# Values scaled by the positive softmax sum as they leave PSUM, and a new written-out order, in a linear-attention and SwiGLU block

## Chip, cores and metric

The kernel runs on one core of one Trainium2 chip. The metric is the device time of one execution in microseconds; lower is better. A launch is repeated and the median is taken.

## What is computed

One transformer block with conditioning: 2048 tokens of 512 numbers, bf16. Six vectors of 512 come from a small product with `c` and set scale, shift and gate of both halves. The first half is linear attention with 32 heads of 16, whose feature map is a pair of softmaxes over 16 numbers; the second is a SwiGLU feed-forward of width 1376.

```python
    mod = (_silu(c) @ w_mod).reshape(c.shape[0], 6, 1, -1)
    h = _layernorm(x, axis=-1) * (1 + ca) + sa
    # attention on h: q, k, v = split(h @ wqkv) in 32 heads of 16
    pq = jnp.einsum('bhsd,hdf->bhsf', q, w_phi)
    pk = jnp.einsum('bhsd,hdf->bhsf', k, w_phi)
    phi_q = jnp.concatenate([_softmax(pq, axis=-1), _softmax(-pq, axis=-1)], axis=-1)
    phi_k = jnp.concatenate([_softmax(pk, axis=-1), _softmax(-pk, axis=-1)], axis=-1)
    kv = jnp.einsum('bhsf,bhsd->bhfd', phi_k, v)
    z = jnp.einsum('bhsf->bhf', phi_k)
    num = jnp.einsum('bhqf,bhfd->bhqd', phi_q, kv)
    den = jnp.einsum('bhqf,bhf->bhq', phi_q, z)[..., None] + 1e-06
    o = num / den
    # x = x + ga * (o @ wo); then the same norm with cb, sb, and
    # x = x + gb * ((silu(h @ w_gate) * (h @ w_up)) @ w_down)
```

## The kernel before

The 2048 tokens are 16 tiles of 128 (`NT`), in four chunks of 512 columns. The two weights `wq` and `wk` are first multiplied by the block-diagonal matrix of `w_phi` (`fold_phi`, L507): each 128-row block is transposed (`wk` on TensorE, L518; `wq` by a DMA transpose through `transposed`, L292, into `WT`), multiplied (L529) and written back (L532, L533).

**First norm.** `first_norm` (L541) takes statistics on VectorE (L348, L349), the reciprocal root (`rstd_lnexp`, on ScalarE L377 or GpSimd L381) and normalizes x to `xn` (L392 to L398). `first_T` (L556) turns `xn` so that the 512 features lie on the partitions, `hT`, and applies scale and shift. Chunk 0 is turned on TensorE, two tiles at a time (`modulate_T`, L403); chunks 1 to 3 by DMA transposes into `raw` (L563), with the scaling after it on VectorE, ScalarE or GpSimd (L571 to L575).

**Key side.** `k_tile` (L595) makes, for one tile, K (L602) and V (L606) in PSUM. ScalarE writes exp(K) and exp(-K) side by side to `e` (L613), 1024 numbers a token. V is copied out of PSUM to `va` with a constant column of ones behind each of eight groups of 64 (L619). VectorE sums `e` in groups of 16 to S, 64 sums a token (L623); R is 1/S, by VectorE (L629) or as exp(-ln S) on ScalarE (L627, L628); GpSimd multiplies all of `e` by R (L631). `kv_tile` (L635) then adds the tile's product of `e` with `va` to an accumulator in PSUM, in eight groups of 65 columns (L638), 64 of values and one of z. After all tiles `f_kvz` (L746) masks it to `KVZ`.

**Query side.** `q_tile` (L653) does the same for Q (L661, L665, L669) but keeps the positive half unscaled, and multiplies the negative half by the ratio of the two sums, `Rq` (L671 to L677), since `o` is a quotient. A DMA transpose puts it into `pT` (L681). `attend_tile` (L773) multiplies `pT` with `KVZ` (L782), divides (L785, L786); `turn`, `project` (L815) with `wo` (scaled by the gate, L738), the residual (L818) and the second norm follow; then the feed-forward: `ffn_gu` (L867, L874, L877, L883), `ffn_tail` (L907, L917), `ffn_down` (L939, L950, L954), output L959.

**What sets the order.** The kernel doesn't issue as it is written. Each step is recorded as an operation with one to three alternatives (engine, cost in the planner's us, function). `ORDER` is a written-out list of the number 4 x operation + alternative: it says in which order operations are given their places and which engine takes each. `Plan.run` (L168) goes through it with the costs, puts each operation at a start, chooses the buffer slots, and issues all in the order of these starts. An engine works through its queue in that order. SyncE's queue (called XBAR) holds all loads and all DMA transposes, at most eight under way at a time. An alternative marked `DVE*` is also kept clear of GpSimd. PSUM is two banks of accumulator and six single banks that all steps share. Where TensorE would pause, `fill` (L989) puts in matmuls on a tensor of ones whose result isn't used (L1006).

## Time and profile before

| what | value |
|---|---|
| median of 13 runs | 207.28 us (205.28 to 208.26) |
| profiled execution, device time | 207.72 us |
| its span, first to last instruction | 205.9 us |
| TensorE busy | 194.3 us, 94% |
| VectorE busy | 143.1 us, 69% |
| GpSimd busy | 127.4 us, 62% |
| ScalarE busy | 109.2 us, 53% |
| first K product on TensorE starts | 14.41 us |

A page of the profile lists engines as PE (TensorE matmuls), PEld (their weight loads), DVE (VectorE), ACT (ScalarE), POOL (GpSimd) and SP (SyncE; SPq is its queue of DMA issues). L602 is line 602 of the kernel. A group such as `one_ps<-wk,hT 128x512 x64` names what is written and read, the shape and the count; behind it stand the busy time, the mean of one in ns, and the idle time of the engine just before, with what ended it. Matmuls overlap, so a group's length on PE is more than the time it takes from the next one; the distance of starts tells that. The chain that ended last is followed back from the last instruction through what released each step.

### The profile page before, as it was taken

Reading aid. Unit: us, or ns where it says so; the run is one execution under the profiler, and the core shown is the slowest. Engines: PE = TensorE matmul, PEld = TensorE weight load, DVE = VectorE, ACT = ScalarE, POOL = GpSimd, SP = SyncE. Lnnn points to the kernel's source line nnn. Section 1 sums busy time; section 2 is a strip of 40 time slices with the busy share of each in tenths; the row PEclk is TensorE's granted clock in tenths of the full one; section 3 lists DMA queues with packets and bytes.
Section 4 is the critical chain, followed back from the end, with each engine's and each line's share of the span. In section 5 each row is a group of like instructions: output and inputs, shape, how many; then the busy total and the mean of one; then the engine's idle time right before and its main releaser. Section 6 shows DMA issues by size and latency. Waiting matters only on the chain.

```text
span 205.9 us, 4577 instructions
## 1 busy us (share of the span) xinstructions
PE 194.3 (94%) x1761; PEld 131.5 (64%) x1761; DVE 143.1 (69%) x284; ACT 109.2 (53%) x221; POOL 127.4 (62%) x180
## 2 busy tenths in 40 slices
PE   7499889999887999999999999999999999999994
PEld 3274365545353597788667866578768688765852
DVE  7699978999998899999987976855324141150533
ACT  2199989999697785456425443425224134332310
POOL 3488986889794767798896585646450860240242
PEclk9999999999999999999999999999999999999999
DMA  5999999994217647483938855041100000101212
GB/s 159 381 376 253 266 193 309 212 377 151 47 29 76 127 80 133 97 148 63 181 76 155 105 99 121 3 103 37 51 29 0 25 30 0 38 16 38 74 31 64
DMA packets 52136, 24.47 MB, mean 119 GB/s; under 512 B 43313, under 2 KB 48914, under 8 KB 52114
## 3 DMA queue, kind: packets, MB, share of 16 engines
q1 hardware_dynamic: 51968, 24.11, 49.9%
q8 instruction: 14, 0.23, 0.5%
q10 hardware_dynamic: 146, 0.07, 0.1%
q14 instruction: 8, 0.07, 0.1%
HBM read 11.58 MB, written 2.10 MB: 66 GB/s over the span
## 4 chain that ended last, share of the span: by engine, by line
PE 65%; DMA 11%; ACT 7%; POOL 5%; DVE 5%; SPq 3%; issue 3%; DVEq 0%; POOLq 0%; ACTq 0%
PE one_ps L867 29%; PE one_ps L939 18%; DMA pT<-eq 6%; PE one_ps L815 6%; DMA wk<-in_A_wqkv_dram 3%; ACT e L613 3%; PE one_ps L661 3%; PE one_ps L907 2%; PE one_ps L602 2%; POOL e L631 2%; ACT hT L573 2%; ACT va L619 2%; POOL eq L677 2%; PE kv_ps L782 1%; SPq L292 1%
## 5 line engine op out<-in xcount | busy, mean ns | idle before, releaser
L867 PE MATMUL one_ps<-hT,wgu_sb 128*128 128x256 bf16 (+1 forms) x800 | 75.6, 251 | 0.1
L867 PEld LDWEIGHTS <-wgu_sb 128*128 128x128 bf16 x800 | 65.5, 98 | 9.2 <-issue 0.2
L874 ACT ACTIVATE sg<-one_ps 128x512 bf16<-128x512 f32 (+1 forms) x42 | 23.5, 573 | 37.1 <-PE one_ps L867 30.5
L939 PE MATMUL one_ps<-wd_sb,gu 128*128 128x512 bf16 (+2 forms) x176 | 39.9, 372 | 0.0
L883 POOL TENSOR_TENSOR gu<-usb,sg 128x512 bf16<-128x512 bf16 x16 | 18.8, 1178 | 33.3 <-ACT usb L881 21.4
L877 DVE TENSOR_TENSOR gu<-one_ps,sg 128x512 bf16<-128x512 f32 (+1 forms) x26 | 16.6, 639 | 26.6 <-PE one_ps L867 12.3
L631 POOL TENSOR_TENSOR e<-e,R 128x1024 bf16<-128x1024 bf16 x16 | 31.0, 1956 | 5.3 <-DVE R L629 4.6
L939 PEld LDWEIGHTS <-gu 128*128 128x128 bf16 (+1 forms) x187 | 17.8, 98 | 16.0
L950 DVE TENSOR_TENSOR fg<-one_ps,gab 128x512 bf16<-128x512 f32 (+1 forms) x16 | 10.6, 665 | 17.6 <-PE one_ps L939 17.6
L348 DVE BATCH_NORM_STATS2 st<-x_c 128x6 f32<-128x512 bf16 x32 | 21.4, 681 | 1.8 <-DMA x_c<-in_A_x_dram 1.6
L669 DVE TENSOR_REDUCE Sq<-eq 128x64 f32<-128x1024 bf16 x16 | 19.0, 1191 | 0.0
L881 ACT CAST usb<-one_ps 128x512 bf16<-128x512 f32 x16 | 9.4, 585 | 17.8 <-PE one_ps L867 17.8
L623 DVE TENSOR_REDUCE S<-e 128x64 f32<-128x1024 bf16 x16 | 18.6, 1184 | 0.1
L665 ACT ACTIVATE eq<-one_ps 128x512 bf16<-128x512 f32 x32 | 17.2, 624 | 1.8 <-PE one_ps L661 1.8
L613 ACT ACTIVATE e<-one_ps 128x512 bf16<-128x512 f32 x32 | 17.6, 659 | 0.1
L677 POOL TENSOR_TENSOR eq<-eq,Rq 128x512 bf16<-128x512 bf16 x15 | 15.8, 1059 | 0.9 <-DVE Rq L672 0.5
L815 PE MATMUL one_ps<-wo_sb,oT 128*128 128x512 bf16 x64 | 15.8, 379 | 0.0
L606 PE MATMUL one_ps<-wv,hT 128*128 128x512 bf16 x64 | 15.8, 379 | 0.0
L602 PE MATMUL one_ps<-wk,hT 128*128 128x512 bf16 x64 | 15.6, 379 | 0.0
L661 PE MATMUL one_ps<-wq,hT 128*128 128x512 bf16 x64 | 15.4, 379 | 0.0
L818 DVE TENSOR_TENSOR x_c<-x_c,one_ps 128x512 bf16<-128x512 bf16 x16 | 10.9, 680 | 5.9 <-PE one_ps L815 5.8
L954 POOL TENSOR_TENSOR ot<-x_c,fg 128x512 bf16<-128x512 bf16 x8 | 9.2, 1152 | 7.5 <-DVE fg L950 7.5
(113 smaller groups left out, 261.8 us busy)
## 6 DMA issues: line engine op xcount, KB each, us to landing
wmod_sb<-in_w_mod_dram SPq DMA_DIRECT2D x2, 1024.0 KB, 7.3
out_dram<-ot SPq DMA_DIRECT2D x15, 128.0 KB, 1.9
...
```

Of the source, the lines that this page charges most:

```text
L348: pl.op("DVE", r=reads, w=[st6], us=0.6, fn=lambda: nc.vector.bn_stats(st6()[:], src))
L602: nc.tensor.matmul(pk()[:], lhsT=hT[c_i][k][:, cols], rhs=Wk2[:, k, :], start=(k == 0), stop=(k == KD - 1))
L613: nc.scalar.activation(e()[:, :, sg].rearrange("p g h f -> p g (h f)"), pk()[:].rearrange("p (g n) -> p g n", g=G), ACT.Exp, scale=(1.0, - ...
L631: pl.op("POOL", r=[e, R], w=[e], us=1.92, fn=lambda: nc.gpsimd.tensor_tensor(e()[:].rearrange("p g s h f -> p (g s h) f"), e()[:].rearrang ...
L661: nc.tensor.matmul(pq()[:], lhsT=hT[c_i][k][:, cols], rhs=Wq2[:, k, :], start=(k == 0), stop=(k == KD - 1))
L669: pl.op("DVE", r=be, w=[Sq], us=1.14, fn=lambda: nc.vector.tensor_reduce(Sq()[:].rearrange("p g s h -> p (g s h)"), eq[:].rearrange("p g s ...
L677: eng.tensor_tensor(eq[:, :, 1], eq[:, :, 1], Rq()[:].unsqueeze(3).to_broadcast([P, G, 4, DH]), op=ALU.mult)
L815: nc.tensor.matmul(a()[:], lhsT=oT()[:, j0 + j, :], rhs=wo_sb[:, j, :], start=(j == 0), stop=(j == KD - 1))
L867: nc.tensor.matmul(ps_()[0:fsz, q * n:(q + 1) * n], lhsT=wgu_sb[:, k, i, m * P:m * P + fsz], rhs=h2[k], start=(k == 0), stop=(k == KD - 1))
L874: pl.op("ACT", r=[g, btab], w=[sg], us=0.08 + 0.41 * L / CW, fn=lambda: nc.scalar.activation(sg()[0:fsz, 0:L], g()[0:fsz, 0:L], ACT.Silu))
L883: pl.op("POOL", r=[usb, sg], w=[gu], us=0.17 + 0.98 * L / CW, fn=lambda: nc.gpsimd.tensor_tensor(gu()[0:fsz, 0:L], usb()[0:fsz, 0:L], sg() ...
L939: nc.tensor.matmul(fp()[:], lhsT=b()[0:fsz, c0:c0 + P], rhs=wd_[0:fsz, m, wcs], start=(m == 0), stop=(m == FM - 1))
```

## The change

- **Key side.** V is multiplied by R of the positive half (1/S+) as it leaves PSUM, on VectorE, instead of being copied; the four columns of z behind each group become R of the positive half (copied on GpSimd or ScalarE) instead of one constant column. The positive half of `e` stays as it is; GpSimd multiplies only the negative half, by S+ x R-, which a small product on GpSimd makes first. The quotients are the same. The accumulator's groups have 68 columns instead of 65, and `f_kvz` reads four z columns per group.
- **First loads and first norm.** x of chunk 0 comes in one load instead of two, x of chunk 1 in two instead of one. Chunk 0 is turned tile by tile (`turn_tile`) and `hT` of chunk 0 is tracked tile by tile; the first two tiles of chunk 1 are turned on TensorE as well instead of by a DMA transpose.
- **Planner's costs.** DMA sizes and the costs of DMA transposes are changed, `Rq` (the product) has only GpSimd as an alternative.
- **Order.** `ORDER` is a new list throughout, so places, engines and slots of all steps are dealt anew. By count of the built program: the 64-wide R, 13 on VectorE and 3 on ScalarE before, are all on ScalarE; SyncE issues x of chunk 1 (first half), x of chunk 0, `w_phi`, `wk`, modulation, x of chunk 1 (second half), modulation, `wq`, x of chunk 2, `wv`, two transposes of `wq`, x of chunk 3, the other two. Before, it was x0a, `w_phi`, x0b, x1, `wk`, two modulation loads, x2, `wv`, x3, `wq`, and transposes after that.

```diff
--- before.py
+++ after.py
@@ -39,51 +39,51 @@
-PAIRS = (0, 1)
-DMA_LN1 = (1, 2, 3)
+DMA_LN1 = 6
 FILL_FROM, FILL_TO, FILL = 1.3, 90.0, 0.85
 
 
 ORDER = [
-    0, 44, 48, 8, 52, 20, 28, 56, 4, 12, 148, 68, 100, 116, 16, 132, 76, 72, 64, 172, 80, 164, 85, 256, 176, 36, 168, 88, 180, 60, 152, 98, 248, 94,
...
+    20, 44, 0, 48, 8, 56, 4, 64, 148, 12, 52, 264, 272, 116, 164, 24, 268, 276, 16, 168, 280, 172, 76, 176, 68, 181, 284, 290, 80, 72, 152, 294, 60,
...
@@ -124,7 +124,7 @@
     OWN = {"PE": 0.0, "DVE": 0.19, "ACT": 0.19, "POOL": 0.12, "SP": 0.0, "XBAR": 0.0, "NONE": 0.0}
-    DMA = (1.9, 385e3, 0.5)
+    DMA = (1.9, 385e3, 0.5, 0.7, 1.3, 1.0)
     LANES = 8
@@ -190,8 +190,8 @@
             elif o.eng == "XBAR" and o.kb == 0:
-                dma = max(dma, o.end + 0.1) + 0.5
-                o.end = max(o.end, dma + 0.6)
+                dma = max(dma, o.end + 0.1) + self.DMA[4 if o.alt[1] > 1.32 else 3]
+                o.end = max(o.end, dma + self.DMA[5])
             elif o.kb < 0:
@@ -316,7 +316,7 @@
     gul_t = [const.tile([P, 2, P], BF16, name=f"gul{i}") for i in range(slots["gul"])]
-    va_t = [const.tile([P, G, HG + 1], BF16, name=f"va{i}") for i in range(slots["va"])]
+    va_t = [const.tile([P, G, NDW], BF16, name=f"va{i}") for i in range(slots["va"])]
     bm4 = const.tile([P, HG], FP32, name="bm4")
@@ -324,9 +324,6 @@
             nc.gpsimd.memset(t[:, :, lastf:P], 0.0)
-        for t in va_t:
-            nc.gpsimd.memset(t[:, :, HG:HG + 1], 1.0)
-
         nc.gpsimd.tensor_tensor(bm4[:], bm128[:, 0:4, :].rearrange("p c f -> p (c f)"),
@@ -338,7 +335,7 @@
     bwgu = [Buf(), Buf()]
-    bc, bphi = Buf(at=2.5), Buf()
+    bc, bphi = Buf(at=2.75), Buf()
     bWq2 = [Buf() for _ in range(KD)]
@@ -428,17 +425,17 @@
-    later(x_ch[0][:, 0:2, :], x_v[0][:, 0:2, :], bx[0:2], 256)
-    later(Wk2[:], wqkv_v[:, :, D:2 * D], bwk[0:1], 594)
-    later(wphi_sb[:], A_w_phi.rearrange("h (q t) f -> (h q) (t f)", t=4), [bphi], 200)
+    later(x_ch[0][:], x_v[0], bx[0:4], 512)
+    later(Wk2[:], wqkv_v[:, :, D:2 * D], bwk[0:1], 560)
+    later(wphi_sb[:], A_w_phi.rearrange("h (q t) f -> (h q) (t f)", t=4), [bphi], 80)
     for k in (0, 2):
         later(wmod_sb[:, k:k + 2, 0:2 * D], wmod_v[:, k:k + 2, 0:2 * D], bm1[k:k + 2], 512)
-    later(x_ch[0][:, 2:4, :], x_v[0][:, 2:4, :], bx[2:4], 256)
-    later(wv_sb[:], wqkv_v[:, :, 2 * D:3 * D], [bwv], 594)
-    later(x_ch[1][:], x_v[1], bx[4:8], 512)
-    later(Wq2[:], wqkv_v[:, :, 0:D], bwq[0:1], 594)
+    later(x_ch[1][:, 0:2, :], x_v[1][:, 0:2, :], bx[4:6], 256)
+    later(x_ch[1][:, 2:4, :], x_v[1][:, 2:4, :], bx[6:8], 256)
+    later(wv_sb[:], wqkv_v[:, :, 2 * D:3 * D], [bwv], 560)
+    later(Wq2[:], wqkv_v[:, :, 0:D], bwq[0:1], 640)
     for c_i in (2, 3):
-        later(x_ch[c_i][:], x_v[c_i], bx[c_i * TPC:(c_i + 1) * TPC], 512)
+        later(x_ch[c_i][:], x_v[c_i], bx[c_i * TPC:(c_i + 1) * TPC], 540)
@@ -502,7 +499,7 @@
     bmask = Buf()
-    pl.op("POOL", w=[bmask], us=1.2, fn=f_masks)
+    pl.op("POOL", w=[bmask], us=0.6, fn=f_masks)
@@ -533,7 +530,7 @@
     hT = [[attn.tile([P, CW], BF16, name=f"hT_{c_i}_{j}") for j in range(KD)] for c_i in range(NCH)]
-    bhT = [[[Buf() for _ in range(KD)] for _ in range(2 if c_i in PAIRS else 1)] for c_i in range(NCH)]
+    bhT = [[[Buf() for _ in range(KD)] for _ in range((4, 2, 1, 1)[c_i])] for c_i in range(NCH)]
@@ -553,14 +550,33 @@
+    def turn_tile(xn, parts, q, t):
+        tp = bank("T", [P, KD, P], BF16)
+
+        def ft():
+            for j in range(KD):
+                nc.tensor.transpose(tp()[:, j, :], xn()[:, q, j * P:(j + 1) * P], ident_b[:])
+        pl.op("PE", r=[xn, parts[q]], w=[tp], us=0.224, fn=ft)
+        for jp in range(2):
+            def evac(act, jp=jp):
+                for j in (2 * jp, 2 * jp + 1):
+                    d = hT[0][j][:, t * P:(t + 1) * P]
+                    if act:
+                        nc.scalar.activation(d, tp()[:, j, :], ACT.Identity, bias=modA[:, j:j + 1], scale=modA[:, KD + j:KD + j + 1])
+                    else:
+                        nc.vector.tensor_scalar(d, tp()[:, j, :], modA[:, KD + j:KD + j + 1], modA[:, j:j + 1],
+                                                op0=ALU.mult, op1=ALU.add)
+            pl.op([("ACT", 0.6, lambda evac=evac: evac(True)), ("DVE", 0.5, lambda evac=evac: evac(False))],
+                  r=[tp, bmodA], w=bhT[0][t][2 * jp:2 * jp + 2])
+
     def first_T(n0, w):
         c_i, t = divmod(n0, TPC)
-        if c_i in DMA_LN1:
+        if n0 >= DMA_LN1:
             raw = sb("prep", "raw1", [P, TPC, KD, P], BF16)
             parts = [Buf() for _ in range(w // 2)]
             for q in range(w // 2):
                 xn, ps2, _ = bxn1[n0 + 2 * q]
-                pl.op("XBAR", r=[xn] + ps2, w=([raw] if q == 0 else []) + [parts[q]], us=1.8, fn=lambda q=q, xn=xn: nc.sync.dma_start(
+                pl.op("XBAR", r=[xn] + ps2, w=([raw] if q == 0 else []) + [parts[q]], us=1.4, fn=lambda q=q, xn=xn: nc.sync.dma_start(
                     raw()[:, 2 * q:2 * q + 2].rearrange("p q j m -> p (q j) m"), xn()[:].rearrange("p q m -> p (q m)"), transpose=True))
@@ -574,9 +590,13 @@
                             d, s, ab, sh, op0=ALU.mult, op1=ALU.add), j))],
-                      r=[raw] + parts + [bmodA], w=[bhT[c_i][t // 2 if c_i in PAIRS else 0][j]])
+                      r=[raw] + parts + [bmodA], w=[bhT[c_i][(t, t // 2, 0, 0)[c_i]][j]])
             return
-        bd = bhT[c_i][t // 2 if c_i in PAIRS else 0]
+        if c_i == 0:
+            for q in range(w):
+                turn_tile(*bxn1[n0 + q], t + q)
+            return
+        bd = bhT[c_i][t // 2]
         for jp in range(2):
@@ -586,11 +606,11 @@
-    bphik, bva, kv_ops = {}, {}, []
+    bphik, bva, bz_, kv_ops = {}, {}, {}, []
         c_i, t = divmod(i, TPC)
-        return bhT[c_i][t // 2 if c_i in PAIRS else 0]
+        return bhT[c_i][(t, t // 2, 0, 0)[c_i]]
@@ -615,31 +635,35 @@
         bva[i] = Buf("va", lambda slot: va_t[slot])
-        def fva(copy):
-            copy(bva[i]()[:, :, 0:HG], v()[:].rearrange("p (g d) -> p g d", g=G))
-        pl.op([("ACT", 0.48, lambda: fva(nc.scalar.copy)), ("DVE", 0.6, lambda: fva(nc.vector.tensor_copy))],
-              r=[v], w=[bva[i]])
-        Ss, R = sb("kph", "S", [P, 2 * H], FP32), sb("kph", "R", [P, 2 * H], FP32)
+        Ss, R = sb("kph", "S", [P, G, 2, 4], FP32), sb("kph", "R", [P, G, 2, 4], FP32)
         pl.op("DVE", r=[e], w=[Ss], us=1.14, fn=lambda: nc.vector.tensor_reduce(
-            Ss()[:], e()[:].rearrange("p g s h f -> p (g s h) f"), axis=AX.X, op=ALU.add))
+            Ss()[:].rearrange("p g s h -> p (g s h)"), e()[:].rearrange("p g s h f -> p (g s h) f"), axis=AX.X, op=ALU.add))
         def fr():
             nc.scalar.activation(R()[:], Ss()[:], ACT.Ln)
             nc.scalar.activation(R()[:], R()[:], ACT.Exp, scale=-1.0)
         pl.op([("DVE", 0.46, lambda: nc.vector.reciprocal(R()[:], Ss()[:])), ("ACT", 0.52, fr)], r=[Ss], w=[R])
+        bz = bz_[i] = Buf()
+        pl.op("POOL", r=[R, Ss], w=[Ss], us=0.22, fn=lambda: nc.gpsimd.tensor_tensor(
+            Ss()[:, :, 0], Ss()[:, :, 0], R()[:, :, 1], op=ALU.mult))
+        pl.op("DVE", r=[v, R], w=[bva[i]], us=0.65, fn=lambda: nc.vector.tensor_tensor(
+            bva[i]()[:, :, 0:HG].rearrange("p g (h d) -> p g h d", d=DH), v()[:].rearrange("p (g h d) -> p g h d", g=G, d=DH),
+            R()[:, :, 0].unsqueeze(3).to_broadcast([P, G, 4, DH]), op=ALU.mult))
+        pl.op([("POOL", 0.17, lambda: nc.gpsimd.tensor_copy(bva[i]()[:, :, HG:NDW], R()[:, :, 0])),
+               ("ACT", 0.24, lambda: nc.scalar.copy(bva[i]()[:, :, HG:NDW], R()[:, :, 0])),
+               ("DVE*", 0.1, lambda: nc.vector.tensor_copy(bva[i]()[:, :, HG:NDW], R()[:, :, 0]))], r=[R, bva[i]], w=[bz])
         bphik[i] = e
-        pl.op("POOL", r=[e, R], w=[e], us=1.92, fn=lambda: nc.gpsimd.tensor_tensor(
-            e()[:].rearrange("p g s h f -> p (g s h) f"), e()[:].rearrange("p g s h f -> p (g s h) f"),
-            R()[:].unsqueeze(2).to_broadcast([P, 2 * H, DH]), op=ALU.mult))
+        pl.op("POOL", r=[e, Ss], w=[e], us=1.02, fn=lambda: nc.gpsimd.tensor_tensor(
+            e()[:, :, 1], e()[:, :, 1], Ss()[:, :, 0].unsqueeze(3).to_broadcast([P, G, 4, DH]), op=ALU.mult))
     def kv_tile(i):
         def f():
             for g in range(G):
-                nc.tensor.matmul(kv_acc(g // 4)[:, (g % 4) * P:(g % 4) * P + HG + 1],
+                nc.tensor.matmul(kv_acc(g // 4)[:, (g % 4) * P:(g % 4) * P + NDW],
                                  lhsT=bphik[i]()[:, g].rearrange("p s h f -> p (s h f)"),
                                  rhs=bva[i]()[:, g, :], start=(i == 0 and g % 4 == 0), stop=(i == NT - 1),
                                  skip_group_check=True)
-        o = pl.op("PE", r=[bphik[i], bva[i], bmask], w=[bkv], us=0.27, fn=f)
+        o = pl.op("PE", r=[bphik[i], bva[i], bz_[i], bmask], w=[bkv], us=0.27, fn=f)
         kv_ops.append(o)
@@ -669,8 +693,7 @@
         pl.op("DVE", r=[Sq], w=[Rq], us=0.28, fn=lambda: nc.vector.reciprocal(Rq()[:], Sq()[:, :, 1]))
-        pl.op([("DVE*", 0.12, lambda: nc.vector.tensor_tensor(Rq()[:], Rq()[:], Sq()[:, :, 0], op=ALU.mult)),
-               ("POOL", 0.22, lambda: nc.gpsimd.tensor_tensor(Rq()[:], Rq()[:], Sq()[:, :, 0], op=ALU.mult))],
+        pl.op([("POOL", 0.22, lambda: nc.gpsimd.tensor_tensor(Rq()[:], Rq()[:], Sq()[:, :, 0], op=ALU.mult))],
               r=[Rq, Sq], w=[Rq])
@@ -678,7 +701,7 @@
         bpT[n] = pT
-        pl.op("XBAR", r=be, w=[pT], us=1.8, fn=lambda: nc.sync.dma_start(
+        pl.op("XBAR", r=be, w=[pT], us=1.4, fn=lambda: nc.sync.dma_start(
             pT()[:], eq[:].rearrange("p g s h f -> p (g s h f)"), transpose=True))
@@ -710,7 +733,7 @@
         cols = slice((2 + 2 * i) * D, (4 + 2 * i) * D)
-        later(wmod_sb[:, :, cols], wmod_v[:, :, cols], [bm2[i]], 1024)
+        later(wmod_sb[:, :, cols], wmod_v[:, :, cols], [bm2[i]], 1200)
     for i in range(NT):
@@ -745,7 +768,7 @@
         src = kv_ps[:].rearrange("p b (g n) -> p (b g) n", n=P)
-        nc.vector.scalar_tensor_tensor(KVZ[:, :, HG:NDW], in0=src[:, :, HG:HG + 1].to_broadcast([P, G, 4]), scalar=0.5 * DEN_EPS,
+        nc.vector.scalar_tensor_tensor(KVZ[:, :, HG:NDW], in0=src[:, :, HG:NDW], scalar=0.5 * DEN_EPS,
                                        in1=bm4z[:].unsqueeze(1).to_broadcast([P, G, 4]), op0=ALU.add, op1=ALU.mult)
@@ -802,7 +825,7 @@
         else:
-            pl.op("XBAR", r=[o] + parts, w=[oT], us=0.82 + 0.49 * w, fn=lambda: nc.sync.dma_start(
+            pl.op("XBAR", r=[o] + parts, w=[oT], us=1.23 + 0.08 * w, fn=lambda: nc.sync.dma_start(
                 oT()[:, 0:w * KD], o()[:, 0:w].rearrange("p q m -> p (q m)"), transpose=True))
@@ -826,7 +849,7 @@
             xn, parts = bxn2[n0]
-            pl.op("XBAR", r=[xn] + parts, w=[raw], us=0.82 + 0.49 * w, fn=lambda: nc.sync.dma_start(
+            pl.op("XBAR", r=[xn] + parts, w=[raw], us=1.23 + 0.08 * w, fn=lambda: nc.sync.dma_start(
                 raw()[:, 0:w].rearrange("p q j m -> p (q j) m"), xn()[:, 0:w].rearrange("p q m -> p (q m)"), transpose=True))
@@ -1001,7 +1024,7 @@
             else:
-                dst = kv_ps[:, 0, :].rearrange("p (g n) -> p g n", n=P)[:, :, HG + 1:P]
+                dst = kv_ps[:, 0, :].rearrange("p (g n) -> p g n", n=P)[:, :, NDW:P]
                 src = src.rearrange("p (g n) -> p g n", g=4)
@@ -1010,7 +1033,7 @@
         else:
-            n, each = (CW, 0.216) if late else (4 * (P - HG - 1), 0.108)
+            n, each = (CW, 0.216) if late else (4 * (P - NDW), 0.105)
             fns += [lambda: f(n)] * int((o.start - t0 - 0.1) * FILL / each)
```

## The prediction

> **What bounds the kernel now.** I read the busy shares first, then TensorE's timeline, then the groups of instructions by shape, last SyncE's queue. The page's shares and the chain that ended last:
>
> ```profile
> PE 194.3 (94%) x1761; PEld 131.5 (64%) x1761; DVE 143.1 (69%) x284; ACT 109.2 (53%) x221; POOL 127.4 (62%) x180
> ...
> PE 65%; DMA 11%; ACT 7%; POOL 5%; DVE 5%; SPq 3%; issue 3%; DVEq 0%; POOLq 0%; ACTq 0%
> ```
>
> TensorE leads, but its busy time hides how dense it is. The timeline (start, length, then the group) gives that by the distance of starts: four matmuls of 512 columns show 1.03 and the next group starts 0.865 later.
>
> ```profile
> 14.41 1.03 PE L602 MATMUL one_ps<-wk,hT 128*128 128x512 bf16 x4
> ...
> 24.77 0.24 PE L471 MATMUL one_ps<-silucT,wmod_sb 128*128 128x1 bf16 x4
> 26.36 0.45 PE L471 MATMUL one_ps<-silucT,wmod_sb 128*128 128x1 bf16 x12 [1.35 <-DMA wmod_sb<-in_w_mod_dram]
> ...
> 55.07 1.03 PE L606 MATMUL one_ps<-wv,hT 128*128 128x512 bf16 x4
> 57.59 0.68 PE L638 MATMUL kv_ps<-va,e 128*128 128x65 bf16 x16 [1.49 <-ACT va L619]
> ...
> 58.96 0.39 PE L1006 MATMUL kv_ps<-ones 128*128 128x252 bf16 x2
> ...
> 63.15 0.39 PE L801 MATMUL one_ps<-ident_b,o 128*128 128x128 bf16 x4
> 64.75 0.43 PE L782 MATMUL kv_ps<-KVZ,pT 128*128 128x68 bf16 x8 [1.21 <-DMA pT<-eq]
> ```
>
> and further on
>
> ```profile
> 71.53 0.81 PE L1006 MATMUL one_ps<-ones 128*128 128x512 bf16 x3
> ...
> 80.28 1.06 PE L867 MATMUL one_ps<-hT,wgu_sb 128*128 128x128 bf16 x16
> 81.54 0.43 PE L782 MATMUL kv_ps<-KVZ,pT 128*128 128x68 bf16 x8 [0.20 <-DMA pT<-eq]
> ```
>
> From the first K product at 14.41 to the last matmul near 202.9 TensorE runs without a break except here. Holes, from the end of one group's dense time to the next start: 24.87 to 26.36 is 1.49 (a wait for the modulation weights); 55.93 to 57.59 is 1.66 (for `va` and the scaled `e`); 63.37 to 64.75 is 1.38; 81.17 to 81.54 is 0.37; one at 119.68 is 0.25: **5.15 us**. Filler matmuls on `ones` take 0.22 at 58.96 and 0.65 (to 72.18): 0.87. So 6.0 of 188.5 us are no work, and the 14.4 ahead are loads and the folding of `Wk2`. The change can win what it takes from these two; engines beside TensorE count only where they open a hole.
>
> The rows that price the edits (busy us, mean ns, idle before), and two of SyncE's queue:
>
> ```profile
> L631 POOL TENSOR_TENSOR e<-e,R 128x1024 bf16<-128x1024 bf16 x16 | 31.0, 1956 | 5.3 <-DVE R L629 4.6 <-PE kv_ps L638 0.7
> L623 DVE TENSOR_REDUCE S<-e 128x64 f32<-128x1024 bf16 x16 | 18.6, 1184 | 0.1
> L786 DVE TENSOR_TENSOR o<-kv_ps,A 128x512 bf16<-128x512 f32 x16 | 10.8, 677 | 0.1
> L629 DVE RECIPROCAL R<-S 128x64 f32<-128x64 f32 x13 | 6.9, 533 | 0.2
> ```
>
> ```profile
> 2.58 0.43 SPq L289 DMA_DIRECT2D wk<-in_A_wqkv_dram  x1
> ...
> 18.82 7.31 SPq L292 DMA_TRANSPOSE WT<-wq  x4
> ```
>
> **What the Trainium skill says.** "Perfetto Trace Analysis", Identifying the Most-Contended Engine: matmul busy share misjudges TensorE because matmuls are pipelined. Agrees: 379 ns each, a start every 216. "VectorE: DVE Perf Modes", the perf-mode tier table: a `tensor_tensor` with a PSUM operand runs in the slow mode. Agrees: L786 takes 677 ns, the bf16 ones from SBUF 429 (L954). "SBUF — State Buffer", SBUF: two separate sides: a VectorE operation with two SBUF inputs and a GpSimd operation exclude each other for a whole instruction. Agrees: at 50.03 the 128x32 `Rq` product (L672) took 1.91 us beside L631 on GpSimd, where GpSimd does it in 0.25. "DMA: Bandwidth & Descriptors", Queues, rings and completion order: completion is not first in, first out. Agrees: `wk`, issued at 2.58, landed after 6.9 us, when the DMA view had 2.45 MB moved, while it and all ahead of it are 1.6 MB.
>
> **Part by part.** *Key side, GpSimd.* L631 halves to 128x512; the same shape on eq (L677) takes 1059 ns: 16 x (1.96 - 1.06) = 14.4 us off. Added: 16 products of 128x32 at 0.25 (L673) = 4.0, 8 copies of 128x32, between 0.10 (memset L312) and 0.25, taken 0.2 = 1.6. From the built order GpSimd also gets five 512-wide `hT` evictions (0.77, as L398) and three more `wo` products (1.16), 7.3. Sum -1.5, the rest cancels to within 1: no relief in total, but the step from R to a ready `e` falls from 1.96 to 1.31.
>
> *Key side, VectorE and ScalarE.* The V copy (15 on ScalarE at 0.48, one on VectorE) becomes 16 VectorE products from PSUM: the L786 row, 0.61 from start to start. Bounds: 0.57 (the VectorE copy it replaces, 25.17 to 25.74) and 0.68 (no overlap), -0.6 to +1.1 in all; only one input is in SBUF, so GpSimd can't hold it. The 13 reciprocals move to ScalarE as Ln and Exp, 0.51 a pair (48.56 to 49.07). ScalarE: -7.2 + 6.6, eight z copies at 0.24 (+1.9) and a few more norms (+2): about +3. VectorE from the first `hT` eviction to `KVZ`, by the new order: 16 S at 1.12, 16 V at 0.61, 4 Sq at 1.12, 3 Rq at 0.26, 8 statistics at 0.62 and 10 aggregations at 0.08, `hT` 2.7 (0.25 each at 128 wide, 71.72 to 72.22), rest 0.4: **41.9 us**; before it was 13.17 to 59.95, 46.8. No `Rq` product is left on VectorE, so the 1.83 us in the chain at 50.1 goes.
> The new wait: each V product waits for R from ScalarE, and behind it on VectorE stand the next S and the statistics, for which ScalarE, GpSimd and TensorE wait in turn.
>
> *TensorE.* The accumulation widens from 65 to 68 columns: nothing (L782, 68 wide, and L638, 65 wide, both take 0.26 per eight). Eight more transposes; one tile's four (0.22) come after the first K product. Fillers after it: one of 240 columns and one of 512, 0.10 + 0.22. Walking the new order at 0.865 per product (four matmuls), 0.26 per `kv` group, 0.22 per fold and 0.78 for modB from the first K at 14.4 ("wanted" below is a step's place in this walk), the last `kv` group ends 41.6 us later, at 56.0; the last S, R, V chain on VectorE ends at 13.2 + 41.9 - 1.1 = 54.0. They fit by 2 us.
>
> *Start.* `wk` moves from fifth to fourth issue with 256 KB less ahead: 0.45 + 0.6 earlier, so about 8.8, between 8.3 and 9.5 (it shares the engines with both modulation loads, which come no earlier). But ScalarE has a Ln pair and a norm before its three `wk` evictions: 0.45 to the first `WT` copy (as from 9.5 to 9.98), 1.45 + 0.5 + 0.7 + 1.45, and 0.7 for the first tile's `hT`: 14.05. On VectorE `modA` stays at 13.05, and a `wk` eviction (0.6) and two `hT` halves (0.5) now stand behind it: 14.15. With 0.2 to the start the first K comes at 14.4, as now: **0, from -0.5 to +0.8**.
>
> *SyncE.* `wq` goes out before x2, wv and x3; its four transposes come before raw, two ahead of x3, all ahead of the gate loads. One took 1.3 of queue (2.8 once) and 4.6 to land: with `wq` there near 13, folds are ready from 17.6, wanted from 18.1 (after four K and a turned tile, 3.7). Gate loads near 19.7 plus 8 is 27.7; modB is wanted at 29.9, so the first hole closes. x3 near 19.5, wanted by VectorE's statistics at 21.3. All hidden, by 0.5 to 2.2; if each comes 2 late, the folds cost some 1.5 and x3 0.5.
> *Later.* eq3, which opened the hole at 63.4, is scaled near 45, its transpose lands near 50, wanted at 59.9. `wo` on GpSimd ends near 60.2 (after the last `e` near 54.5, one eq, four at 1.16), wanted at 61.1. Here Sq adds 2 x 1.12 on VectorE, and four `hT` evictions and three `wo` products that leave (4.3) pay for it.
>
> **The sum.** Removed 5.15 + 0.87; added 0.32 + 0.22: -5.5 if nothing new opens. New holes I expect: `hT` of chunk 2, wanted at 36.3 (its last `xn` stands on GpSimd behind 10 us of work that starts with the first R at 20.4; transpose from 30.4, landing 34.5, three evictions of 0.77 to 36.9): 0.6; folds 0.4; end of the key stage 0.8 (VectorE has 2 us in 42 to spare, no wait counted); elsewhere 0.6: 2.4, bounds 0 to 4.9. Net **-3.1**. The profiled execution took 207.72 (span 205.9, 1.8 around it): 204.6. It lies 0.44 above the median of the 13 runs; taken off 207.28, **204.2**.
>
> **Rivals.** *All closed* (0.15): 207.28 - 5.5 = 201.8. For it: all margins but that of chunk 2 are positive. Against: most are under 2 us, and before, a queue that was laid as tightly opened five holes.
> *Loads take the holes' place* (0.24): folds, x3 and gate loads come as late as they landed before (four transposes took 7.3 us of queue): 2.5 on top of 2.4: 206.7, half of it within the same.
> *VectorE becomes the bound; slower* (0.11): each of 16 V products finds R unfinished behind two exponentials on ScalarE (0.97) and holds its queue. At 0.5 us each, 8 us come in, 2 fit into the slack and 5.5 are won elsewhere only in part (3.1 kept): 207.28 + 8 - 2 - 3.1 = 210.2. It decides from 0.39 a product (16 x 0.39 = 6.2, less 2 and 3.1, is 1.0). For it: the view by stages has ScalarE 95 to 100% busy from 10 to 50. Against: in the new order VectorE has one to three other operations between an S and its V product, 1 to 3 us in which ScalarE can finish R.
> *Not as it says:* GpSimd's sum barely falls, so the halved product alone wins nothing; that lies in the forecast.
>
> **How the numbers follow.** Forecast 204.2 (0.50). Range 201.8 to 207.4: it takes in the closed case and the loads. What a measurement can tell from no change is 0.5%, 1.04 us. Faster 0.50 + 0.15 + 0.12 = 0.77, same 0.12, slower 0.11.
>
> **What would show it.** Right: first K within 14 to 15.2, `KVZ` near 56 to 57.5, no hole over 1 us at modB or before the second attend, the dense stretch ending near 200. Wrong: first K after 15.5, folds waiting for `WT`, or VectorE idle before L649 (after) for ScalarE in most of its 16.

## The result and the profile after

After: **202.53 us** median of 11 runs (201.77 to 204.53), against 206.79 for the kernel before in 48 runs (205.28 to 208.59). The ratio is 0.9819, with a 95% interval of 0.9789 to 0.9849: 3.7 us less, between 3.1 and 4.4 (the two medians differ by 4.3). The profiled execution took 202.49 (span 200.7), so it stands at the median; that of before (207.72) stood 0.9 above its own.

The page of after, its busy shares and the chain that ended last:

```profile
PE 194.6 (97%) x1767; PEld 131.7 (66%) x1767; DVE 137.2 (68%) x277; ACT 109.9 (55%) x244; POOL 125.5 (63%) x211
...
PE 85%; ACT 5%; DMA 5%; DVE 2%; issue 1%; SPq 1%; ACTq 0%; DVEq 0%
```

TensorE does the same 194 us of work, but it now makes up 85% of the chain instead of 65%: DMA fell from 11 to 5%, GpSimd left the chain. TensorE's timeline of after (start, length, group, and what ended an idle time before it), first to the second attend product:

```profile
13.63 1.07 PE L622 MATMUL one_ps<-wk,hT 128*128 128x512 bf16 x4
...
17.36 0.39 PE L526 MATMUL one_ps<-BD,WT 128*128 128x128 bf16 x4
17.94 2.00 PE L626 MATMUL one_ps<-wv,hT 128*128 128x512 bf16 x8 [0.20 <-ACT e L633]
...
29.54 0.42 PE L662 MATMUL kv_ps<-va,e 128*128 128x68 bf16 x8
29.80 0.94 PE L468 MATMUL one_ps<-silucT,wmod_sb 128*128 128x1 bf16 x32
...
55.49 0.26 PE L1029 MATMUL kv_ps<-ones 128*128 128x240 bf16 x1
55.59 0.42 PE L662 MATMUL kv_ps<-va,e 128*128 128x68 bf16 x8
...
59.77 0.42 PE L805 MATMUL kv_ps<-KVZ,pT 128*128 128x68 bf16 x8
```

and further on:

```profile
70.99 1.05 PE L890 MATMUL one_ps<-hT,wgu_sb 128*128 128x128 bf16 x16
72.69 1.04 PE L838 MATMUL one_ps<-wo_sb,oT 128*128 128x512 bf16 x4 [0.65 <-DMA oT<-o]
```

All 32 matmuls of modB now follow one `kv` group without a wait (29.80), the last `kv` groups need no more waiting, and the second attend starts without one (59.77). What opened anew is small: 0.36 at 17.6 (a V product that waits for ScalarE's `e`) and 0.22 at 19.7 (a fold; the trace names nothing that it waits for), 0.24 at 65.7, and **0.81** before 72.69, where a `wo` product waits for `oT`. With pieces of some 0.1 that is 1.8 us.

The same in two stretches. The lines give start and end, length, busy time of TensorE, its weight loads, VectorE, ScalarE and GpSimd (with instructions), the granted clock, DMA share and GB/s. The first stretch runs from the first K product to `KVZ` and is called the key stage below. Before:

```profile
14.41:59.95 45.54, 42.64 (x346) 22.39 (x345) 42.81 (x72) 42.94 (x90) 39.07 (x30) 1.00 0.84 212
59.95:205.90 145.95, 141.40 (x1297) 102.92 (x1295) 89.09 (x179) 59.96 (x119) 80.39 (x123) 1.00 0.36 72
```

After:

```profile
13.63:56.04 42.41, 42.21 (x347) 22.25 (x347) 41.32 (x71) 38.92 (x104) 37.77 (x66) 1.00 0.92 234
56.04:200.70 144.66, 140.82 (x1296) 102.83 (x1294) 86.06 (x174) 63.78 (x124) 81.33 (x126) 1.00 0.38 70
```

The key stage lost 3.1 us, and TensorE's records leave 0.2 of it uncovered (before 2.9). The rest lost 1.3 in this pair of profiles, which is the hole before the second attend. The start seems to have lost 0.8, but that is chance, as the runs below show. VectorE is idle 1.1 us in the new key stage. ScalarE is busy 4.0 us less there, where the prediction had about 3 more.

The rows that price the edits, from the groups by shape:

```profile
L656 POOL TENSOR_TENSOR e<-e,S 128x512 bf16<-128x512 bf16 x16 | 16.9, 1059 | 0.3
L639 DVE TENSOR_REDUCE S<-e 128x64 f32<-128x1024 bf16 x16 | 19.3, 1205 | 0.8 <-ACT e L633 0.7 <-POOL e L656 0.2
L649 DVE TENSOR_TENSOR va<-one_ps,R 128x512 bf16<-128x512 f32 x16 | 10.7, 677 | 0.0
L643 ACT ACTIVATE R<-S 128x64 f32<-128x64 f32 x16 | 4.3, 266 | 0.7 <-DVE S L639 0.7
```

The product on GpSimd costs 1.06 as forecast, and no V product stood idle before it started (0.0): R was there each time. SyncE's queue:

```profile
2.11 0.43 SPq L289 DMA_DIRECT2D wk<-in_A_wqkv_dram  x1
...
12.78 3.27 SPq L292 DMA_TRANSPOSE WT<-wq  x2
...
16.73 2.51 SPq L292 DMA_TRANSPOSE WT<-wq  x2
...
20.67 1.16 SPq L289 DMA_DIRECT2D wmod_sb<-in_w_mod_dram  x2
```

The four transposes of `wq` now precede both gate loads; before they followed both, and took 7.3 us of the queue. modB, the gate loads' reader, starts 9.1 us after their issue.

### The profile page after: what moved, and what is told of

It reads as the page before. It is cut to its first block, busy times and chain, and to the rows that moved or that the text cites. A ratio compares the mean times of both kernels' runs of the same rounds, so it can differ in the third digit from the quotient of the medians.

```text
span 200.7 us, 4670 instructions
## 1 busy us (share of the span) xinstructions
PE 194.6 (97%) x1767; PEld 131.7 (66%) x1767; DVE 137.2 (68%) x277; ACT 109.9 (55%) x244; POOL 125.5 (63%) x211
## 4 chain that ended last, share of the span: by engine, by line
PE 85%; ACT 5%; DMA 5%; DVE 2%; issue 1%; SPq 1%; ACTq 0%; DVEq 0%
PE one_ps L890 33%; PE one_ps L962 18%; PE one_ps L626 7%; PE one_ps L838 6%; PE one_ps L622 5%; PE one_ps L685 5%; DMA wk<-in_A_wqkv_dram 3%; ACT eq L689 3%; PE one_ps L930 3%; PE kv_ps L662 2%; DMA oT<-o 2%; PE kv_ps L805 2%; PE one_ps L717 1%; PE one_ps L468 1%; PE one_ps L526 1%; ACT hT L565 1%
## 5 line engine op out<-in xcount | busy, mean ns | idle before, releaser
L890 PE MATMUL one_ps<-hT,wgu_sb 128*128 128x256 bf16 (+1 forms) x800 | 76.9, 251 | 0.0
L962 PE MATMUL one_ps<-wd_sb,gu 128*128 128x512 bf16 (+2 forms) x176 | 40.9, 372 | 0.0
L639 DVE TENSOR_REDUCE S<-e 128x64 f32<-128x1024 bf16 x16 | 19.3, 1205 | 0.8 <-ACT e L633 0.7
L689 ACT ACTIVATE eq<-one_ps 128x512 bf16<-128x512 f32 x32 | 16.7, 611 | 2.0 <-PE one_ps L685 2.0
L633 ACT ACTIVATE e<-one_ps 128x512 bf16<-128x512 f32 x32 | 17.0, 613 | 0.6 <-PE one_ps L622 0.6
L700 POOL TENSOR_TENSOR eq<-eq,Rq 128x512 bf16<-128x512 bf16 x16 | 16.8, 1058 | 0.5
L656 POOL TENSOR_TENSOR e<-e,S 128x512 bf16<-128x512 bf16 x16 | 16.9, 1059 | 0.3
L838 PE MATMUL one_ps<-wo_sb,oT 128*128 128x512 bf16 x64 | 16.3, 379 | 0.6 <-DMA oT<-o 0.6
L977 POOL TENSOR_TENSOR ot<-x_c,fg 128x512 bf16<-128x512 bf16 x7 | 8.1, 1170 | 6.3 <-DVE fg L973 6.3
```

The costliest lines, as they stand in the source:

```text
L639: pl.op("DVE", r=[e], w=[Ss], us=1.14, fn=lambda: nc.vector.tensor_reduce(Ss()[:].rearrange("p g s h -> p (g s h)"), e()[:].rearrange("p g ...
L689: pl.op("ACT", r=[pq, btab], w=[be[sg]], us=0.48, fn=lambda sg=sg: nc.scalar.activation(eq[:, :, sg].rearrange("p g h f -> p g (h f)"), pq ...
L838: nc.tensor.matmul(a()[:], lhsT=oT()[:, j0 + j, :], rhs=wo_sb[:, j, :], start=(j == 0), stop=(j == KD - 1))
L890: nc.tensor.matmul(ps_()[0:fsz, q * n:(q + 1) * n], lhsT=wgu_sb[:, k, i, m * P:m * P + fsz], rhs=h2[k], start=(k == 0), stop=(k == KD - 1))
L962: nc.tensor.matmul(fp()[:], lhsT=b()[0:fsz, c0:c0 + P], rhs=wd_[0:fsz, m, wcs], start=(m == 0), stop=(m == FM - 1))
```

## The experiments

Each of the twelve is timed against the kernel before, on the same chip. The table has the profiled executions, one for each kernel: first K product, start of `KVZ`, the key stage between them, the rest of the span. The profile of b_loads lies 1.9 us above the median of its runs and that of b_mod_later 1.2 below; the ratios are of all runs.

| kernel | ratio to before (95%) | first K | `KVZ` | key stage | rest |
|---|---|---|---|---|---|
| before | 1 | 14.41 | 59.95 | 45.5 | 145.9 |
| after | 0.982 (0.979 to 0.985) | 13.63 | 56.04 | 42.4 | 144.7 |
| b_half | 0.988 (0.985 to 0.992) | 13.49 | 58.60 | 45.1 | 144.8 |
| b_gate | 1.001 (0.998 to 1.003) | 13.17 | 60.87 | 47.7 | 144.7 |
| b_loads | 1.008 (1.005 to 1.010) | 18.02 | 62.56 | 44.5 | 146.0 |
| b_prod | 1.051 (1.045 to 1.056) | 13.37 | 71.56 | 58.2 | 144.7 |
| b_mod_later | 1.001 (0.998 to 1.004) | 13.14 | 59.57 | 46.4 | 144.5 |
| b_half_mod | 0.999 (0.995 to 1.002) | 13.45 | 61.26 | 47.8 | 144.1 |
| b_half_all | 0.998 (0.996 to 1.000) | 13.27 | 60.10 | 46.8 | 144.7 |
| a_both | 1.070 (1.064 to 1.076) | 13.40 | 71.76 | 58.4 | 147.1 |
| a_recip | 1.008 (1.006 to 1.011) | 13.07 | 60.95 | 47.9 | 144.9 |
| a_v_extra | 0.991 (0.988 to 0.994) | 13.35 | 58.80 | 45.5 | 144.1 |
| a_two_banks | 0.978 (0.973 to 0.983) | 13.18 | 55.59 | 42.4 | 144.8 |
| a_wo_later | 0.979 (0.974 to 0.983) | 14.05 | 56.46 | 42.4 | 144.2 |

In all of them the filler matmuls are those of the kernel they start from. My theory was that each hole has its own cause and its length is what it is worth. The rivals were that one engine's relief (GpSimd's halved product) makes the gain, that the value product does, or that the start does.

### The halved product alone (b_half)

```diff
-            e()[:].rearrange("p g s h f -> p (g s h) f"), e()[:].rearrange("p g s h f -> p (g s h) f"),
-            R()[:].unsqueeze(2).to_broadcast([P, 2 * H, DH]), op=ALU.mult))
+            e()[:, :, 1], e()[:, :, 1],
+            R()[:].rearrange("p (g s h) -> p g s h", g=G, s=2)[:, :, 1].unsqueeze(3).to_broadcast([P, G, 4, DH]), op=ALU.mult))
```

> The kernel before, in its own order, with GpSimd scaling only the negative half of each e (it leaves out the scaling of the positive half): the product falls from 1.96 to about 1.06 us, 14.4 us less GpSimd work in the key stage, nothing else moved. Theory (the gain comes from single waits, each with its own cause): of the holes only the third, 1.38 before the second attend (eq3 scaled by GpSimd behind the products), can close and a part of the second; total -1.2 us, between -0.5 and -2, with the hole at modB unchanged at 1.5. Rival (the halved product is what makes the change faster): -3 us or more. A third case, GpSimd never last: within 0.4.

Measured: 0.988, 2.4 us less, between 1.7 and 3.2: between the two theories. TensorE's timeline of this run, at the places of the second and third hole:

```profile
54.68 1.03 PE L606 MATMUL one_ps<-wv,hT 128*128 128x512 bf16 x4
56.24 0.68 PE L638 MATMUL kv_ps<-va,e 128*128 128x65 bf16 x16 [0.53 <-ACT va L619]
...
61.80 0.39 PE L801 MATMUL one_ps<-ident_b,o 128*128 128x128 bf16 x4
62.03 0.42 PE L782 MATMUL kv_ps<-KVZ,pT 128*128 128x68 bf16 x8
```

The third hole is gone and the second fell from 1.65 to 0.70; the one at modB stayed (1.54). In the profile the key stage and the rest lost 1.6 together; a new wait of 0.7 near 19.5 (K for GpSimd's `hT`) took a part back. So GpSimd's product was part of the path in the kernel before, though GpSimd was busy only 39 of 45.5 us there; what shows it is the timed 2.4, not the two holes, which also close where the product is whole (next run). The key stage stays 2.7 us longer than that of after.

### The gate loads alone (b_gate)

```diff
 SyncE's order
-  wmod gate load, transpose raw<-xn, wmod gate load, four transposes WT<-wq
+  wmod gate load, wmod gate load, transpose raw<-xn, four transposes WT<-wq
```

> The kernel before with one DMA moved: the second load of the gate weights goes out right after the first, ahead of a transpose. No other engine's order changes. Theory: modB's matmuls at 24.8 find their weights and the first hole (1.49 us) closes; -1.0 us in all, between -0.6 and -1.6. Rival (the end of the key stage is set by ScalarE and VectorE, 44.1 of 46.8 us busy each): the hole closes and the one before the last kv groups (1.66) grows by as much; within 0.4.

Measured: 1.001, nothing gained. TensorE's timeline of this run:

```profile
23.91 0.24 PE L468 MATMUL one_ps<-silucT,wmod_sb 128*128 128x1 bf16 x4
24.64 0.45 PE L468 MATMUL one_ps<-silucT,wmod_sb 128*128 128x1 bf16 x12 [0.48 <-DMA wmod_sb<-in_w_mod_dram]
26.09 0.40 PE L526 MATMUL one_ps<-BD,WT 128*128 128x128 bf16 x4 [0.99 <-DMA WT<-wq]
...
29.92 0.61 PE L526 MATMUL one_ps<-BD,WT 128*128 128x128 bf16 x4 [1.03 <-DMA WT<-wq]
```

The wait for the modulation weights shrinks to 0.48, and the folds right behind it now wait for `WT`, because the four transposes stand later in SyncE's queue (20.1 in place of 18.8). Neither theory had this: the hole was shared, and one named wait hid the next. The granted clock fell here as well, which the last section comes to.

The second and the third hole are gone as well, though GpSimd's product is whole. The second attend of this run:

```profile
64.37 0.39 PE L798 MATMUL one_ps<-ident_b,o 128*128 128x128 bf16 x4
64.59 0.42 PE L779 MATMUL kv_ps<-KVZ,pT 128*128 128x68 bf16 x8
```

The same holds for b_mod_later below, and the rest of the span takes 144.7 and 144.5 in the two, as in b_half (144.8) and after. TensorE lost time earlier, and what it waited for later had then arrived. So the holes depend on each other, and one that closes late in the key stage doesn't tell which edit closed it.

### The first loads alone (b_loads)

```diff
 SyncE's first loads
-  x0 half, wphi, x0 half, x1, wk, wmod, wmod, x2, ...
+  x0 half, x0 half, wphi, wk, wmod, x1 half, wmod, x1 half, x2, ...
```

> The kernel before with only its first loads in the order of after: x0 in two halves first, then wphi, wk, the first modulation weights, half of x1, the second modulation weights, the other half of x1; norms, transposes and every engine's order as before. Theory (the start's gain is 256 KB that no longer stand ahead of the second modulation load, and wk a place earlier): modA about 0.9 earlier, near 12.0, and the first K product 0.6 earlier, near 13.8 (13.4 to 14.1); total -0.5. Rival (the regrouped first norms and the single turned tiles did it): first K within 0.2 of 14.4, total 0.

Measured: 1.008, 1.6 us slower, against both theories. This profile is a late one (1.9 above the median of its runs, and TensorE's granted clock averaged 0.81 up to the first K at 18.02), so its waits may be longer than usual. VectorE's timeline:

```profile
9.65 0.69 DVE L345 BATCH_NORM_STATS2 st<-x_c 128x6 f32<-128x512 bf16 x1 [3.23 <-DMA x_c<-in_A_x_dram]
```

`wk` was there at 7.7. But VectorE, in its old order, stood 3.2 us before a statistic of x1, which now lands later, and `BD`, the norm's scale and ScalarE's `WT` copies stood behind it. The edit also isn't the order of after, as its expectation has it: after issues the first half of x1 ahead of everything, this run behind `wk` and the first modulation load. So the run shows what a late x1 costs in the old order of norms; what the loads of after are worth alone wasn't measured.

### The product alone (b_prod)

```diff
-        pl.op([("ACT", 0.48, lambda: fva(nc.scalar.copy)), ("DVE", 0.6, lambda: fva(nc.vector.tensor_copy))], ...)
+        pl.op("DVE", r=[v, R], w=[bva[i]], us=0.65, fn=lambda: nc.vector.tensor_tensor(..., op=ALU.mult))
+        (behind R, which is Ln and Exp on ScalarE for all 16; GpSimd: S*R, then the negative half of e)
```

> The kernel before with the product of the change alone: V divided on VectorE on leaving PSUM, all 16 reciprocals on ScalarE, GpSimd scaling the negative half by S times R; the order of before, with steps moved only where a PSUM buffer needs it, and the loads of before. It leaves out the sums for three heads in four (one column of R is copied, so the denominators are not right). Theory (the product needs the new order: VectorE gets 9.6 us and gives back 6.9, which makes 46.8 of busy time in a key stage of 46.8): +3 us, between 0 and +8, with VectorE waiting for ScalarE's R. Rival (the product brings the gain by itself): -2 us or more.

Measured: 1.051, 10.5 us slower, above the expected range. VectorE's waits from 13 to 72 us (what waited for what: us in total, times, longest):

```profile
DVE va L624 <- ACT R L621: 9.8, 8, 3.0
DVE va L624 <- PE one_ps L603: 1.9, 2, 1.1
```

This is the mechanism of the prediction's third rival: the V product finds R unfinished on ScalarE and holds VectorE's queue. In after the same product waits 0.0. The product is the same, so what stands around it, the order above all (loads and first norms differ too), decides whether it costs 10 us or nothing. (The order was only made to fit, with the fewest moves, and the granted clock averaged 0.91 in this key stage, so the 10.5 is more than the waits alone would cost in a good order.)

### modB later (b_mod_later, b_half_mod)

```diff
 TensorE's order
-  V, modB k0 k1, fold, modB k2, fold, kv, gate rows, modB k3, fold, K, kv, fold, V, K, kv, kv, q
+  V, fold, fold, kv, K, kv, V, K, kv, modB k0 to k3, fold, fold, gate rows, kv, q
```

> The kernel before with modB's 32 matmuls, the gate rows' four and two folds of wq placed some 4 us later in TensorE's order, behind two K products and a V product, so that the gate loads (landing at 26.3) and WT have arrived; loads and all else as before. Theory (holes add up, each is worth its own length): the hole of 1.49 goes and -1.3 us in all, between -0.9 and -1.6. Rival (GpSimd's product of 1.96 sets the end of the key stage, as the run with the halved product suggests): the hole goes, the one before the last kv groups grows by most of it, and the total falls by 0.5 at most.

> The kernel before with both: GpSimd scales only the negative half of e (it leaves out the scaling of the positive half), and modB's matmuls, the gate rows and two folds stand some 4 us later on TensorE. The halved product alone gave 0.9882 of before, 2.4 us. Both theories of the later modB meet here, since GpSimd is relieved: -3.7 us (2.4 and 1.3), between -3.0 and -4.2, which is what the whole change gives. Rival (the gain of the change needs its new order and its value product elsewhere): no more than the halved product gives alone, -2.4 within 0.4.

Measured: 1.001 and 0.999. Neither theory holds: modB waits no more, and nothing is won; on top of the halved product, the 2.4 us are even lost. TensorE's timeline of b_mod_later:

```profile
21.56 2.75 PE L603 MATMUL one_ps<-wv,hT 128*128 128x512 bf16 x12
26.29 0.88 PE L526 MATMUL one_ps<-BD,WT 128*128 128x128 bf16 x8 [1.97 <-DMA WT<-wq]
```

The two folds that stood behind modB now wait until 26.29, nearly to the moment when the gate loads had come before (26.36). In b_half_mod the same hole is 2.1 us, and after it TensorE ran at half its clock for some 3.4 us (granted 0.69 from 26 to 28, 0.50 to 30, 0.96 to 32):

```profile
27.83 1.90 PE L599 MATMUL one_ps<-wk,hT 128*128 128x512 bf16 x4
29.52 0.65 PE L635 MATMUL kv_ps<-va,e 128*128 128x65 bf16 x8
```

The next start comes 1.69 after the K product's, where 0.865 is the rule.

### All three latecomers (b_half_all)

Beside the gate loads and `WT`, the `hT` of chunk 1's second half was also late. ScalarE's timeline of b_half:

```profile
25.22 1.64 ACT L573 ACTIVATE hT<-raw,modA 128x256 bf16<-128x256 bf16 x3
```

It finished at 26.86, so the steps that need it were no more ready at 24.8 than modB and the folds.

```diff
 TensorE's order
+  V, kv, K, kv, V, K, kv, modB k0 to k3, fold, fold, gate rows, fold, fold, V, kv, q
 ScalarE's order
-  e, va, e, va, va, hT, hT, hT
+  e, hT, hT, hT, va, e, va, va
```

> The kernel before with the halved product (it leaves out the scaling of the positive half of e) and, around the hole at 24.8, everything that waits for the three transfers of that moment placed later or fetched earlier: ScalarE turns chunk 1's second half into hT some 3 us earlier, TensorE does a K, a V and a K product and two kv groups of it first, and modB, all four folds of wq, the gate rows and one V product follow. The runs before it had shown that the gate loads, WT and this hT all arrive between 26.2 and 26.9, so that moving the readers of one only uncovers the next. Theory (one hole, three latecomers; if all three are passed by, the 1.5 us are won on top of the halved product): -3.7 us, between -3.0 and -4.2, close to the whole change. Rival (ScalarE, 95% busy there, has no room: what is put first delays e and va, and the hole comes back within a few us): -2.4 within 0.6, or less.

Measured: 0.998, 0.5 us less than before and 1.9 more than the halved product alone: the rival. TensorE's waits from 14 to 70 us:

```profile
PE kv_ps L635 <- ACT va L616: 1.8, 3, 0.8
PE one_ps L599 <- POOL hT L572: 0.8, 1, 0.8
```

Now the `kv` groups wait for `va`, which ScalarE copies behind the `hT` that was put first. ScalarE itself stood 0.49 us at 23.0 before that `hT`, whose transposed x hadn't landed. The hole has moved, not shrunk: ScalarE has no room there. In after the V copy is not on ScalarE.

### The product undone (a_both)

```diff
+            nc.gpsimd.tensor_tensor(e()[:, :, 0], e()[:, :, 0], unit1[:].unsqueeze(3).to_broadcast([P, G, 4, DH]), op=ALU.mult)
             nc.gpsimd.tensor_tensor(e()[:, :, 1], e()[:, :, 1], Ss()[:, :, 0].unsqueeze(3).to_broadcast([P, G, 4, DH]), op=ALU.mult)
```

> The kernel after with GpSimd multiplying both halves again (the positive half by ones): 16 products of 1.06 us more, 17 us, on an engine that is 39.3 of 44.0 us busy in the key stage. Theory (the halving pays for the work that GpSimd took over, and the order lives from it): +9 us, between +6 and +13, the key stage longer by that. Rival (GpSimd stays off the path): within 1.

Measured: 1.070, 18 us above after, twice what I expected. The key stage, and TensorE's longest waits in it:

```profile
13.40:71.76 58.36, 44.66 (x341) 22.03 (x347) 42.10 (x72) 39.64 (x104) 54.03 (x82) 0.98 0.65 173
```

```profile
PE kv_ps L667 <- POOL e L661: 9.1, 8, 3.2
PE kv_ps L667 <- POOL va L654: 3.9, 3, 1.6
```

Of the 17.1 us that were added on GpSimd, 16.0 lengthen the key stage. By the sum alone 12.5 had to: 37.8 and 17.1 make 54.9, in a stage of 42.4. GpSimd was idle for the other 4.6 us in the key stage of after, but little of that could be used. Its row of the page of after (busy tenths, slices of 5.0 us) shows where the idle time is:

```profile
POOL 3463999999998997889795758472016260440510
```

It lies ahead of 20 us, before the first product has an R; from there to 60 us GpSimd is busy 90% or more.

### VectorE's reserve (a_recip, a_v_extra)

```diff
-            nc.scalar.activation(R()[:], Ss()[:], ACT.Ln)
-            nc.scalar.activation(R()[:], R()[:], ACT.Exp, scale=-1.0)
+            nc.vector.reciprocal(R()[:], Ss()[:])
```

> The kernel after with the 16 reciprocals on VectorE in place of Ln and Exp on ScalarE, in the same places of the order: 16 x 0.46 to 0.53 = 7.4 to 8.5 us more on VectorE, which is idle 1.1 us in the key stage, and 8.2 less on ScalarE. Theory: VectorE bounds the stage at once: +6.5 us, between +5 and +8. Rival (R comes without a hop to another engine, and VectorE's chain shortens by it): +2 at most.

```diff
             R()[:, :, 0].unsqueeze(3).to_broadcast([P, G, 4, DH]), op=ALU.mult)
+            nc.vector.tensor_copy(spare[:], v()[:, 0:192])
```

> The kernel after with one more VectorE copy of 192 columns out of PSUM behind each of the 16 V products, some 0.25 us each, 4.0 in all; its result is used by nothing. It measures the reserve of VectorE that the third rival of the prediction put at 0.39 us a product. Theory (1.1 us idle in the key stage, and no more): +2.9 us, between +2 and +4. Rival (the reserve is 2 us plus what lies ahead of TensorE): within 1.

Measured: 1.008 and 0.991 of before, which is 5.5 and 1.9 us above after (6.3 and 2.5 by the medians); the first lies in the range of the theory, the second at its lower end. Their key stages:

```profile
13.07:60.95 47.88, 43.66 (x341) 22.33 (x348) 47.46 (x87) 33.56 (x72) 38.37 (x66) 1.00 0.83 210
```

```profile
13.35:58.80 45.45, 43.40 (x346) 22.57 (x351) 45.06 (x87) 39.41 (x104) 38.97 (x67) 1.00 0.89 223
```

VectorE's busy time rises from 41.3 to 47.5 and to 45.1, and the stage follows it: 6.1 more busy gave 5.5, and 3.7 more gave 3.0. The reserve is 0.7 us in both. VectorE is idle 0.4 us in each stage: it has become the bound. In after TensorE and VectorE are thus within 1 us of each other as the bound of the key stage.

### Two attempts at more (a_two_banks, a_wo_later)

```diff
-        tp = bank("T", [P, KD, P], BF16)
+        tps = [bank("T", [P, KD, P], BF16) for _ in range(2 if t == 0 else 1)]
```

> The kernel after with the four transposes of the first tile in two PSUM banks in place of one, so that ScalarE and VectorE each read a bank of their own. In after VectorE's first hT half (13.23) stands idle 0.48 us until ScalarE has finished with the same bank. Theory (two engines take turns on one bank here): both halves run side by side, the first K product comes 0.4 us earlier (0.2 to 0.5), the total falls by 0.2 to 0.5. Rival (VectorE waits for something else that ends then): first K at 13.6, total within 0.2.

```profile
12.78 0.59 DVE L566 TENSOR_SCALAR hT<-one_ps,modA 128x128 bf16<-128x128 bf16 x2 [0.34 <-ACT hT L564]
```

The wait named ScalarE again, with a bank for each, so the bank was not its cause; in the run a_recip the same wait names TensorE's transposes. The first K at 13.18 lies in the scatter of after's start. My theory fell.

```diff
 TensorE's order
-  gate product x16, wo product of oT, gate product x8, attend
+  gate product x24, wo product of oT, attend
```

> The kernel after with one wo product moved behind one group of later work on TensorE: in after it waits 0.65 to 0.8 us at 71.9 for the transposed attention output (oT), issued at 68.7 and 4.0 on its way. Theory: this hole closes and nothing new opens: -0.6 us on after, between -0.3 and -0.8, so 0.979 of before. Rival (the work moved ahead of it waits in turn for its own bank or for its hT): within 0.2 of after.

```profile
73.26 1.04 PE L835 MATMUL one_ps<-wo_sb,oT 128*128 128x512 bf16 x4 [0.36 <-DMA oT<-o]
```

The hole fell from 0.81 to 0.53, and the median (202.63) is that of after. A step of 0.4 us was too short, and its worth is below what can be measured. Neither version is faster than after beyond the uncertainty.

## Why the prediction was right, and where not

The sum gave -3.1 us and the time 204.2; measured is -3.7 (3.1 to 4.4) and 202.5, in the range, at its fast side. Of the 1.7 us between the two times 0.5 is the base, since the median of before is 206.8 in 48 runs and was 207.3 in 13. Two signs of being right were not met: the first K came at 13.63, not within 14 to 15.2, and the dense stretch ended at 197.6, not near 200. `KVZ` at 56.04 lies where the walk had it by luck in part: a start that was 0.8 earlier and 0.7 of new holes in the stage cancel.

- **Holes removed:** all three named holes closed, as forecast. They were 5.9, not 5.15: I had left out pieces of 0.15 to 0.22 each. With fillers (0.87 out; 0.32 and a tile's turn, 0.22, in) and 1.8 of new holes the balance is -4.4, which is what the two stretches show (3.1 + 1.3).
- **New holes** were the term that was mis-sized, 2.4 for 1.8. A fold stood 0.22 (0.4 forecast), a V product 0.36 for ScalarE's `e`, which the sum did not name, and "elsewhere" came to 1.05 (0.6). Chunk 2's `hT` (0.6) and the end of the key stage (0.8) cost nothing. Chunk 2's `hT` was complete at 36.06, not 36.9, and its K product started at 36.28, where the walk had it.
- **The start** was forecast at 0, and that holds. Seven executions with the start of before have their first K between 13.14 and 14.41 (median 13.37), six with that of after between 13.07 and 14.05 (median 13.38); b_loads is left out. The -0.78 of the profiled pair is this scatter: the profile of before had the latest start of the seven. The reason given for 0 holds as well: `wk` does land earlier (its first transpose at 7.3 to 8.3, before at 8.3 to 9.6), but from there to the first K it takes 5.7 to 5.9 us instead of 4.8 to 4.9. The prediction had 8.8 and 14.4, which is 5.6.
- **VectorE** at 41.9 us, with 2 us to spare: the new order has it busy 41.3, and the reserve measured is 0.7. It fits, more tightly than I wrote.
- **ScalarE** was forecast about 3 us busier; in the key stage it is 4.0 less busy (42.9 to 38.9). By the rows of the two stages the V copies took 9.4 off and R and z put 8.4 back, near the forecast; but the added norms did not come, and `hT` and `eq` evictions that went to other engines or out of the stage took 2.5 and 1.8 off.
- **"VectorE becomes the bound; slower"** did not occur in after, but its mechanism is real: b_prod shows it at 9.8 us. What I wrote against it (one to three other operations between S and the V product) is what b_prod lacks in its longest waits (3.0 us at 18.0 behind 0.3 us of other work, 2.1 at 28.6 behind 0.2) and after has. Its point of decision was a little high: with 0.7 us of reserve and 3.7 won, and the same 1.0 to be told from no change, it is 0.34 us a product (5.4 / 16), not 0.39.
- **"All closed"** (201.8) came nearest in size.
- **"The halved product alone wins nothing"** is the step that failed. I set the halving off against the work that GpSimd takes over, as one sum that falls little. Alone, with nothing taken over, the halving gave 2.4 us (GpSimd is busy 26.1 us in that key stage, 39.1 before); undone in after it costs 18, since the work taken over then doesn't fit. That 13 us less on GpSimd give only 2.4 fits a product that stands at the end of each tile's chain, beside other waits; this is argued.
- **The first hole** was closed, but it was not one wait. I took the DMA that the trace names for its cause and its 1.49 us for its price. Gate loads, `WT` and `hT` all came within 0.7 us of each other, and ScalarE had no time to spare there. Four hand-made moves in the old order won nothing from it. The named wait also closed with nothing changed at modB, where TensorE started late: b_loads has no wait at modB, and its holes two and three stand (1.48 and 1.19 us in the trace).

So of the gain of 3.7 us, 2.4 (1.7 to 3.2) come from GpSimd's halved product alone, in the old order and with the old loads: this is shown. The other 1.3 (2.1 by the medians of after and b_half) come with the value product, the new order and the new loads together; in the profiles it is a key stage that is 2.7 us shorter than that of b_half. Each alone, as far as I tried it, loses or wins nothing: the product without the order costs 10 us, and moves of single steps, without V's copy leaving ScalarE, only shift the wait. That ScalarE's relief is what lets the first hole close fits all of this, but it is argued. No run has the new order without the product, or the loads of after alone, so how the remainder divides stays open. The 1.3 us by which the rest of the span is shorter than in the profile of before can't be put down to one edit: b_gate and b_mod_later have a rest as short with the whole product, and before itself has one profile only.
